# Issuing one batch's strided q, k and v two steps later on ScalarE's queue

## The chip, the core and the metric

The kernel runs on one core of a Trainium2 chip. The metric is the device time of one execution in microseconds (us), the median of several runs. TensorE does the matrix products, VectorE (DVE), ScalarE (ACT) and GpSimd (POOL) the rest; transfers are issued by SyncE (SP) and, for four of them in all, by ScalarE. Each engine works through its own instructions strictly in order and waits at an instruction until the semaphores that it names have been counted up.

## The reference, cut to what matters

Eight batches, eight heads, 576 tokens, head size 64. Heads 0 to 3 see the last 32 keys, heads 4 to 7 ("strided") every 32nd key. Attention is followed by a token mixer and a channel mixer with shared weights.

```python
scores = (q @ k.T) / 8
mask_local   = (rel >= 0) & (rel < 32)                    # heads 0-3
mask_strided = (rel >= 0) & (key % 32 == query % 32)      # heads 4-7
x = softmax(where(mask, scores, -1e9)) @ v                # [8, 576, 512]
h = relu(x.T @ w_tok1) @ w_tok2                           # token mixer
u = x + h.T
out = u + relu(u @ w_ch1) @ w_ch2                         # channel mixer
```

## The kernel before

Nearly all products are on TensorE in split precision: an operand is kept as a high and a low part, and three products stand for one. The channel mixer is done in nine groups. A group is one call of `mlp`: for 512 tokens of batch b it runs 12 up-projections (L688, 12 products each, into the tile `h`) and 12 down-projections (L700, 12 products each, into `acc`). Each of these 24 blocks ends with `done()`, which counts a step and then calls whatever was registered for that step with `at(step, function)`. All other work is hung on these steps, and so the order of the instructions on TensorE, VectorE, ScalarE and GpSimd is the order in which the program was written. SyncE's transfers are put in order by the builder, from its own estimate of when each could go.

What the first group (b = 0) carries beside its own blocks:

- `pieces`: most of the weights are still being loaded and split. A piece is a load of 512 KB into `w_raw` (two buffers) or `xhl` (L105, on SyncE's queue), two passes on ScalarE (L115, L118) and two on VectorE (L116, L120) which turn the int64 view into high and low words, then the high part on ScalarE (L129) and the low part on GpSimd (L130). The last six pieces use `w_raw` alone, so each of those loads waits until the piece two before it has been read.
- Batch 1's attention. Its strided heads write their results from `ex` (L361) and its local heads from `lx` (L245) to a tensor `x` in DRAM, `x_83` in the listings below.
- At step 12: `load_next`, which loads batch 1's `x` back into SBUF in six transfers, four for rows 0 to 511 (L452) and two for the rest (L455). At steps 15 to 19 the token mixer's first half follows: each chunk of `x` is cast on ScalarE (L466, into `xhl`), its low part taken on VectorE (L472, and L469 for the short last chunk), and multiplied on TensorE (L484).
- At step 12 as well: `first_ends`. It closes the pool of batch 1's attention, opens the pool `sp` in the same space, and starts the generator `strided` for batch 2. From batch 2 on the strided heads are done on GpSimd (products `sprod`, L372) and VectorE (sums, L418 and L442). The generator first issues the loads of k, q and v, 576 KB each, into three buffers `sa` (L385). For batch 2 alone they are issued from ScalarE's queue; for later batches from SyncE's. Their space was that of `ex`, `lx` and others, so the issue waits for those to be written out.
- From step 16: `some_strided`, which hands out GpSimd's products.

After each block's 12 up-projection products, ScalarE takes `gh` (L691) and VectorE `gl` (L692) out of `h`; there is one `h`, so the next up-projection waits for `gl`.

Transfers are counted on eight semaphores, named DMAHW0 to DMAHW7 in the listings. They are dealt in turn to the transfers of both queues in the order of the program, and a transfer waits until the one eight places before it has landed, unless something earlier has already waited for that.

Of the kernel before, what the change touches and what calls it, by code (L numbers as in the profile page):

```python
# [56 lines left out]
def attn_mixer_kernel(ctx, tc, qkT, vw, qs, ks, vs, qksT, vsP, mask, mask2, w1, w2, wt1, wt2, outT):  # L57
# [391 lines left out]
    def load_x(x_t, b, cs):  # L449
        src = xd[b // 2][S * (b % 2):S * (b % 2) + S, cs]  # L450
        for c in range(NSC - 1):
            nc.sync.dma_start(out=x_t[:, c, cs], in_=src[P * c:P * c + P])  # L452

        for r in range(2):
            nc.sync.dma_start(out=x_t[64 * r:64 * r + 64, NSC - 1, cs], in_=src[P * (NSC - 1):])  # L455
# [39 lines left out]
    def new_h(pool):  # L495
        return [[pool.tile([P, DM], F32R, name=f"h{k}{m}", bufs=1) for k in "hl"] for m in range(2)]
# [8 lines left out]
    def tok2(pool, ps_t, x_t, h, cc, us):  # L505

        cs = slice(P * cc, P * cc + P)
        pu = ps_t.tile([P, 512], F32, name="t")
        for c in range(NSC - 1):
            nc.tensor.matmul(pu[:, P * c:P * c + P], x_t[:, c, cs], ident, is_transpose=True, start=(c == 0), stop=False, skip_group_check=True)  # L510
        yield
        for m in range(2):
            hh, hl = h[m]
            for k, (l, r) in enumerate(((hh, t2h), (hh, t2l), (hl, t2h))):
                nc.tensor.matmul(pu, l[:, cs], r[:, m, :MAIN], start=False, stop=(m == 1 and k == 2), skip_group_check=True)  # L515
        us.append(split_u(pool, pu))
        yield
# [11 lines left out]
    def load_tails(u_t):  # L529

        halves = [xp.tile([P, 2, DM], F32, name="xhl") for _ in range(2)]
        for p in range(B // 2):
            l_t = halves[p // 2][:, p % 2]
            for b in (2 * p, 2 * p + 1):
                rs = slice(TAIL * (b % 2), TAIL * (b % 2) + TAIL)
                nc.sync.dma_start(out=u_t[rs, p], in_=ud[b][:TAIL])
                nc.sync.dma_start(out=l_t[rs], in_=ud[b][TAIL:])
            nc.gpsimd.tensor_tensor(out=u_t[:, p], in0=u_t[:, p], in1=l_t, op=ALU.add)

    def tail_u(pool, ps_t, u_t, cc):  # L540
        pu = ps_t.tile([P, 512], F32, name="t")
        for p in range(B // 2):
            nc.tensor.transpose(pu[:, P * p:P * p + P], u_t[:, p, P * cc:P * cc + P], ident)
        return split_u(pool, pu)
# [187 lines left out]
    def out_group(b):  # L732

        def write(cc, o_t, part):
            queue = nc.scalar if part.start else nc.sync
            queue.dma_start(out=outT[P * cc:P * cc + P, MAIN * b + part.start:MAIN * b + part.stop], in_=o_t[:, part])

        return write
# [14 lines left out]
    def first_ends():  # L753

        for g in lanes + rest:
            assert next(g, lanes) is lanes
        pools.pop("second").__exit__(None, None, None)
        pools["sp"] = ctx.enter_context(tc.tile_pool(name="sp", bufs=1, reuse_waits="tile"))
        turn["gen"] = strided(pools["sp"], NSB)
        turn["owed"] -= next(turn["gen"])  # L760

# [42 lines left out]
    for b in range(B):  # L804
        after = {}

        def at(i, f, *args):
            after.setdefault(i, []).append(lambda: f(*args))

        def load_next(b):  # L810
            x_t = xp.tile([P, NSC, DM], F32, name="x", bufs=1)
            x_next.update(x=x_t, h=new_h(xp), u=[])
            assert turn["batch"] > b or b < NSB, (b, turn)
            load_x(x_t, b, slice(0, DM))
            x_next["tok1"] = tok1(xp, ps_t, x_t, x_next["h"], slice(0, DM))


        def do_tok1():
            next(x_next["tok1"], None)

        def do_tok2(ccs):
            mixes = [tok2(up0, ps_t, x_next["x"], x_next["h"], cc, x_next["u"]) for cc in ccs]
            for g in mixes + mixes:
                next(g)

        def do_tail(cc):
            x_next["u"].append(tail_u(up0, ps_t, x_next["x"], cc))

        at(2 if b == 0 else 0, tok2_tail, ps_t, x_t, h, b)
        if b + 1 < B:  # L830
            at(12, load_next, b + 1)
            steps = (15, 16, 17, 18, 19, 19) if b < 2 else range(14, 20)
            for i in steps:
                at(i, do_tok1)
            for cc in (0, 2):
                at(20 + cc, do_tok2, (cc, cc + 1))
        else:
            x_next.update(x=xp.tile([P, NSC, DM], F32, name="x", bufs=1), u=[])
            at(1, lambda: load_tails(x_next["x"]))
            for cc in range(NCC):  # L840
                at(20 + cc, do_tail, cc)
        if b == 0:
            for i in range(len(pieces)):
                at(int(1.8 * i) / 2, do_pieces, i)
            for k, g in enumerate(lanes):
                for i in range(12):
                    at(i + 0.5 * k, next, g, None)
            for g, steps in zip(rest, ((0, 1.5, 2.5, 3.5), (2, 4.5, 5.5, 6.5), (5, 7.5, 8.5, 9.5), (7, 9.5, 10.5, 11.5)), strict=True):
                for i in steps:
                    at(i, next, g, None)  # L850
            at(12, first_ends)
            at(int(0.9 * len(pieces)) + 1, staging_ends)
        for k, steps in UNITS[b].items():
            for n, i in enumerate(steps):
                if i is not None:
                    at(i, unit, k, n)
        for i in range(24):
            if b or i >= 16:
                at(i, some_strided, 20 if b < 2 else 23)
        mlp(u, after, out_group(b))  # L860
        x_t, h, u = x_next["x"], x_next["h"], x_next["u"]
# [76 lines left out]
```

## Time and profile before

| | |
|---|---|
| median of 3 runs | 821.47 us (820.43 to 827.81) |
| the profiled execution | 818.1 us |
| its span, first to last instruction | 816.3 us |
| TensorE busy | 796.5 us (98%) |
| VectorE, GpSimd, ScalarE busy | 451.1, 410.7, 234.5 us |
| mean granted TensorE clock | 0.992 |

The profiled execution is 1.8 us longer than its span. Times inside the span are counted from its first instruction. A timeline line gives start, duration, engine, code line, operation, the tile written <- the tiles read, and in brackets the idle time before it and what ended that. "SPq" and "ACTq" are instructions that issue a transfer; their duration is that of the issue, not of the transfer.

### The profile page before, as it was taken

What the parts mean: (1) busy time and instruction counts of PE and PEld (TensorE: products, weight loads), DVE (VectorE), ACT (ScalarE), POOL (GpSimd) and SP (SyncE); (2) the same over time, 40 slices, a digit from 0 to 9 for tenths busy, and PEclk for the clock granted to TensorE, in tenths of its full rate; (3) what the DMA queues carried; (4) which work ended last, traced back from release to release, by engine and by line L of the source; (5) the groups of instructions that cost most, each with busy time, mean ns of one, the idle gap of its engine ahead of it and who ended that gap; (6) DMA issues with size and microseconds to landing.
All of it is one profiled execution on the core that took longest, in us unless ns stands there. A gap on an engine that the chain in (4) does not pass through costs nothing.

```text
span 816.3 us, 14373 instructions
## 1 busy us (share of the span) xinstructions
PE 796.5 (98%) x5819; PEld 647.2 (79%) x5823; DVE 451.1 (55%) x991; ACT 234.5 (29%) x491; POOL 410.7 (50%) x309
## 2 busy tenths in 40 slices
PE   9799997999999999999999999999999999999998
PEld 6578675878788888888888888888888888888886
DVE  6867744777587667665856565666562223113112
ACT  5667754232121212132213121322122121111110
POOL 2223334959896696668767866686830101302000
PEclk9999997999999999999999999999999999999999
DMA  9586554233602251137104400542032013001001
GB/s 308 167 274 219 172 174 158 82 136 103 210 1 94 73 180 30 65 93 241 51 13 146 159 30 1 175 160 85 1 94 81 5 46 123 0 1 53 1 0 52
DMA packets 56622, 82.77 MB, mean 101 GB/s; under 512 B 18292, under 2 KB 33396, under 8 KB 56556
## 3 DMA queue, kind: packets, MB, share of 16 engines
q1 hardware_dynamic: 55980, 79.95, 30.3%
q10 hardware_dynamic: 576, 1.90, 0.7%
q8 instruction: 46, 0.75, 0.4%
q14 instruction: 20, 0.16, 0.1%
HBM read 61.32 MB, written 20.38 MB: 100 GB/s over the span
## 4 chain that ended last, share of the span: by engine, by line
PE 89%; DVE 4%; DMA 3%; ACT 1%; issue 1%; SPq 1%; DVEq 0%; ACTq 0%
PE acc L700 34%; PE h L688 31%; PE t L484 6%; PE t L515 5%; PE t L688 3%; PE t L510 1%; DMA x<-x 1%; PE t L296 1%; PE t L268 1%; PE t L334 1%; PE t L524 1%; PE t L286 1%; DVE w_f L120 1%; DMA eqk<-in_qksT 1%; DMA w_raw<-in_w 1%
## 5 line engine op out<-in xcount | busy, mean ns | idle before, releaser
L372 POOL TENSOR_TENSOR sprod<-sa,ss 128x576 f32<-128x576 f32 (+8 forms) x108 | 153.2, 1449 | 75.5 <-issue 39.0
L692 DVE SCALAR_TENSOR_TENSOR gl<-h,gh 128x512 fp32r<-128x512 f32 x99 | 68.3, 690 | 202.6 <-ACT gh L691 202.6
L372 POOL TENSOR_TENSOR sprod<-sa 128x576 f32<-128x576 f32 (+8 forms) x108 | 160.5, 1515 | 33.6 <-DVE ss L418 11.2
L700 PE MATMUL acc<-gh,w2h 128*128 128x512 f32 x432 | 171.7, 397 | 0.0
L700 PE MATMUL acc<-gl,w2h 128*128 128x512 f32 x432 | 169.4, 392 | 0.0
L700 PE MATMUL acc<-gh,w2l 128*128 128x512 f32 x432 | 169.1, 391 | 0.0
L688 PE MATMUL h<-uh,w1h 128*128 128x512 f32 x396 | 157.8, 398 | 1.0 <-DVE gl L692 1.0
L688 PE MATMUL h<-ul,w1h 128*128 128x512 f32 x396 | 154.7, 391 | 0.0
L688 PE MATMUL h<-uh,w1l 128*128 128x512 f32 x396 | 154.5, 390 | 0.0
L691 ACT ACTIVATE gh<-h 128x512 fp32r<-128x512 f32 x99 | 59.1, 597 | 308.1 <-PE h L688 308.0
L372 POOL TENSOR_TENSOR ot<-uh,ul 128x512 f32<-128x512 f32 x36 | 50.3, 1406 | 94.9 <-DVE xhl L472 47.6
L700 PEld LDWEIGHTS acc<-gh,w2h 128*128 128x128 f32 x432 | 81.9, 189 | 17.4
L700 PEld LDWEIGHTS acc<-gh,w2l 128*128 128x128 f32 x432 | 81.8, 189 | 17.4
L700 PEld LDWEIGHTS acc<-gl,w2h 128*128 128x128 f32 x432 | 81.9, 190 | 16.7 <-DVE gl L692 0.3
L688 PEld LDWEIGHTS h<-uh,w1h 128*128 128x128 f32 x396 | 74.3, 188 | 18.1 <-DVE gl L692 1.8
L688 PEld LDWEIGHTS h<-ul,w1h 128*128 128x128 f32 x396 | 74.5, 188 | 15.9
L418 DVE TENSOR_REDUCE ss<-sprod 128x9 f32<-128x576 f32 (+8 forms) x108 | 80.0, 778 | 11.8 <-POOL sprod L372 11.6
L688 PEld LDWEIGHTS h<-uh,w1l 128*128 128x128 f32 x396 | 74.4, 188 | 14.5
L442 DVE TENSOR_REDUCE sa<-sprod 128x64 f32<-128x576 f32 (+8 forms) x108 | 79.4, 776 | 7.9 <-POOL sprod L372 7.8
L484 PE MATMUL t<-xhl,t1h 128*128 128x512 f32 x144 | 45.8, 404 | 7.0 <-ACT xhl L466 6.2
L502 DVE TENSOR_TENSOR ul<-t,uh 128x512 fp32r<-128x512 f32 x36 | 24.8, 690 | 48.7 <-ACT uh L501 48.5
L472 DVE TENSOR_TENSOR xhl<-x,xhl 128x512 fp32r<-128x512 f32 x32 | 36.9, 1173 | 12.9 <-ACT xhl L466 12.9
(123 smaller groups left out, 880.7 us busy)
## 6 DMA issues: line engine op xcount, KB each, us to landing
out_t<-ot SPq DMA_DIRECT2D x35, 256.0 KB
w_raw<-in_w SPq DMA_DIRECT2D x17, 512.0 KB
lqk<-in_qkT SPq DMA_DIRECT2D x20, 416.0 KB
lv<-in_vw SPq DMA_DIRECT2D x20, 390.0 KB
x<-x SPq DMA_DIRECT2D x28, 256.0 KB
xhl<-in_w SPq DMA_DIRECT2D x7, 512.0 KB
x<-lv SPq DMA_DIRECT2D x9, 384.0 KB
x<-sa SPq DMA_DIRECT2D x24, 144.0 KB
```

Source lines behind the costliest of these rows:

```text
L120: nc.vector.scalar_tensor_tensor(out=a, in0=a, scalar=3, in1=y, op0=ALU.logical_shift_left, op1=ALU.bitwise_xor)
L372: i = nc.gpsimd.tensor_tensor(op=op, **operands)
L418: nc.vector.tensor_reduce(out=s_t[:, i, :i + 1], in_=pr.rearrange("p (n d) -> p n d", d=D), axis=AX.X, op=ALU.add)
L442: nc.vector.tensor_reduce(out=o_t[:, i], in_=pr.rearrange("p (d n) -> p d n", n=i + 1), axis=AX.X, op=ALU.add)
L472: apart.append(nc.vector.tensor_tensor(out=xlo, in0=x, in1=xh.bitcast(F32), op=ALU.subtract))
L484: nc.tensor.matmul(ph[m], l[:, c, P * m:P * m + P], r, start=(c == 0 and k == 0), stop=(c == NSC - 1 and k == 1))
L502: nc.vector.tensor_tensor(out=ul, in0=pu, in1=uh.bitcast(F32), op=ALU.subtract)
L515: nc.tensor.matmul(pu, l[:, cs], r[:, m, :MAIN], start=False, stop=(m == 1 and k == 2), skip_group_check=True)
L688: nc.tensor.matmul(ph, l[:, cc, fs], r, start=(cc == 0 and k == 0), stop=(cc == NCC - 1 and k == 2))
L691: nc.scalar.activation(out=gh, in_=ph, func=AF.Relu)
L692: nc.vector.scalar_tensor_tensor(out=gl, in0=ph, scalar=0.0, in1=gh.bitcast(F32), op0=ALU.max, op1=ALU.subtract)
L700: nc.tensor.matmul(acc[cc], l[:, fc, cs], r, start=(fc == 0 and k == 0), stop=(fc == NFC - 1 and k == 2))
```

## The change

The generator for batch 2 is no longer started in `first_ends` at step 12 but in a function of its own at step 14. `first_ends` still closes and opens the pools at step 12.

```diff
@@ first_ends
         pools.pop("second").__exit__(None, None, None)
         pools["sp"] = ctx.enter_context(tc.tile_pool(name="sp", bufs=1, reuse_waits="tile"))
+
+    def first_strided():
         turn["gen"] = strided(pools["sp"], NSB)
         turn["owed"] -= next(turn["gen"])
@@ b == 0
             at(12, first_ends)
+            at(14, first_strided)
             at(int(0.9 * len(pieces)) + 1, staging_ends)
```

ScalarE's queue at that place before, around the three loads of k, q and v (`sa`); `w_raw`, `w_rest`, `w_f`, `w1h` and `w2h` belong to the pieces:

```order
L691 ACTIVATE gh<-h 128x512 [waits PE_49]
L385 DMA sa<-in_ks 128x1152 [waits DMAHW5_49]
L385 DMA sa<-in_qs 128x1152 [waits DMAHW0_49,DMAHW7_49,DVE_49,Activation_49]
L385 DMA sa<-in_vs 128x1152 [waits DMAHW3_49,DMAHW1_49]
L115 ACTIVATE w_rest_92<-w_raw,small 128x512 [waits DMAHW2_49]
L118 ACTIVATE w_f<-w_raw 128x512 [waits Pool_49]
```

ScalarE's queue around the same loads with the change, two steps on, where the next `gh` has been taken and the first cast of `x` (L466) follows:

```order
L691 ACTIVATE gh<-h 128x512 [waits PE_49]
L115 ACTIVATE w_rest_92<-w_raw,small 128x512 [waits DMAHW4_49,Activation_49]
L118 ACTIVATE w_f<-w_raw 128x512 [waits Pool_49]
L129 CAST w1h<-w_f 128x2x256 [waits DVE_49]
L385 DMA sa<-in_ks 128x1152
L385 DMA sa<-in_qs 128x1152 [waits DMAHW5_49,DMAHW0_49]
L385 DMA sa<-in_vs 128x1152 [waits DMAHW6_49,DMAHW3_49]
L466 CAST xhl<-x 128x512 [waits DMAHW3_49]
```

The three loads moved behind nine instructions of the pieces and one `gh`, and now stand directly ahead of the cast. The semaphores that they wait for changed with the place: DMAHW5 and DMAHW6 are now also those of the loads of `x`'s second and third chunk.

SyncE's queue around the loads of batch 1's `x`, the difference (- before, + with the change):

```order
 L245 DMA x_83<-lx 128x2x128
-L452 DMA x<-x_83 128x512 x4
+L452 DMA x<-x_83 128x512
+L105 DMA w_raw<-in_w 128x1024
+L452 DMA x<-x_83 128x512 x3
 L455 DMA x<-x_83 64x512 x2
-L105 DMA w_raw<-in_w 128x1024 x4
+L105 DMA w_raw<-in_w 128x1024 x3
```

The first of the last four weight loads moved from behind all six loads of `x` to behind the first of them. On TensorE, VectorE and GpSimd no instruction moved.

## Rows read from the trace of the kernel before

**Rows 1.** The page: TensorE's clock, in tenths, in 40 slices of 20.4 us.

```profile
PEclk9999997999999999999999999999999999999999
```

**Rows 2.** Waits of TensorE from 120 us to the end: total us, times, longest.

```profile
PE t L484 <- ACT xhl L466: 6.2, 2, 6.0
PE h L688 <- DVE gl L692: 1.0, 2, 0.6
```

**Rows 3.** Timeline of TensorE around the two longest of these waits.

```profile
122.32 0.50 PE L688 MATMUL h<-uh,w1h 128*128 128x512 f32 x1 [0.57 <-DVE gl L692]
...
124.94 0.39 PE L688 MATMUL h<-ul,w1h 128*128 128x512 f32 x1
131.32 0.80 PE L484 MATMUL t<-xhl,t1h 128*128 128x512 f32 x1 [5.99 <-ACT xhl L466]
```

**Rows 4.** Timeline of ScalarE, its issues among them.

```profile
115.56 0.38 ACTq L385 DMA_DIRECT2D sa<-in_ks  x1
...
116.95 0.34 ACTq L385 DMA_DIRECT2D sa<-in_vs  x1
117.35 0.88 ACT L115 ACTIVATE w_rest<-w_raw,small 128x512 uint8<-128x512 uint8 x1 [3.14 <-DMA x<-lx]
...
120.93 0.61 ACT L691 ACTIVATE gh<-h 128x512 fp32r<-128x512 f32 x1
128.86 0.87 ACT L115 ACTIVATE w_rest<-w_raw,small 128x512 uint8<-128x512 uint8 x1 [7.32 <-DMA w_raw<-in_w]
...
130.64 0.62 ACT L466 CAST xhl<-x 128x512 fp32r<-128x512 f32 x1
```

**Rows 5.** Timeline of SyncE's issues.

```profile
116.98 3.55 SPq L452 DMA_DIRECT2D x<-x  x4
120.58 3.91 SPq L455 DMA_DIRECT2D x<-x  x2
124.59 9.92 SPq L105 DMA_DIRECT2D w_raw<-in_w  x4
...
130.26 0.33 SPq L105 DMA_DIRECT2D w_raw<-in_w  x1
```

**Rows 6.** The chain that ended last: start, us, what.

```profile
116.98 6.99 DMA x<-x
...
124.59 4.18 DMA w_raw<-in_w
...
131.32 2.93 PE t L484 x6
134.25 4.34 PE acc L700 x12
138.59 1.37 PE t L484 x6
...
144.04 2.72 PE acc L700 x12
```

**Rows 7.** Windows: length, busy PE PEld DVE ACT POOL, PEclk, DMA share, GB/s.

```profile
99.00:102.00 3.00, 1.24 (x39) 0.90 (x39) 2.90 (x9) 2.43 (x5) 1.38 (x2) 1.00 0.13 20
...
104.00:106.00 2.00, 2.00 (x8) 1.60 (x7) 0.89 (x2) 1.43 (x3) 0.00 (x0) 0.50 0.07 16
...
122.00:125.00 3.00, 2.68 (x12) 2.17 (x12) 0.26 (x1) 0.00 (x0) 1.10 (x1) 1.00 1.00 358
...
131.00:137.00 6.00, 5.68 (x13) 4.46 (x14) 4.52 (x5) 3.85 (x8) 4.08 (x3) 0.50 0.52 173
...
133.00:134.00 1.00, 1.00 (x3) 0.76 (x3) 1.00 (x1) 0.00 (x0) 0.79 (x1) 0.50 0.00 0
```

**Rows 8.** Timeline of GpSimd (first strided product), VectorE and TensorE (last chunk).

```profile
141.08 1.60 POOL L372 TENSOR_TENSOR sprod<-sa 128x576 f32<-128x576 f32 x1
...
146.57 0.69 DVE L469 TENSOR_TENSOR xhl<-x,xhl 64x512 fp32r<-64x512 f32 x1
...
147.51 1.07 PE L484 MATMUL t<-xhl,t1h 128*128 128x512 f32 x4
```

## The prediction

> **What bounds the kernel now.** I read the page first: TensorE is busy for 98% of the span (the table), and its clock is at full level everywhere but in the seventh slice, 122 to 143 us [rows 1]. So time can come only from the few gaps of TensorE and from that slice. The waits of TensorE say where the gaps are: after 120 us it waits 6.2 us in all for the cast of `x` (6.0 at once) and 1.0 us for `gl` [rows 2]. Its timeline puts both big ones beside each other: 0.57 us before the up-projection at 122.32, and 5.99 us before the first token-mixer product at 131.32 [rows 3]. Both lie where the change works, so I went back from them on ScalarE and then on SyncE.
>
> The small one: the up-projection waits for `gl`, this for `gh`, which ScalarE takes only at 120.93. Ahead of `gh` stand six instructions of the pieces, which begin at 117.35 after 3.14 us in which ScalarE issued the three strided loads and waited for the `lx` write to land [rows 4]. The large one: the cast at 130.64 stands behind a piece (L115 at 128.86) that waited 7.32 us for its `w_raw` [rows 4]. That load was issued only at 124.59, since SyncE had all six loads of `x` to issue first, from 116.98 on, and the last two took it 3.91 us [rows 5]. The chain shows why: it waited for a load of `x` issued at 116.98 to land after 6.99 us [rows 6]. A `w_raw` of twice that size landed after 4.18 us [rows 6]; the load of `x` was so slow because the three strided loads (1.77 MB) had been issued just before it and the 16 DMA engines were fully busy (share 1.00, 358 GB/s from 122 to 125) [rows 7]. After the long gap the granted clock is 0.50 from 131 to 137, the lower of its two levels, 1.2 GHz [rows 7].
>
> **The change, part by part.**
>
> *1. The small gap goes.* ScalarE is free from 117.35 - 3.14 = 114.21 instead of 117.35 [rows 4]. The six piece instructions took 120.93 - 117.35 = 3.6 us, so they end near 118, and `gh` can go up to 3.1 us earlier, as soon as its products are through; `gl` follows 0.57 us too late now, so a fifth of that is enough. Worth 0.57 us [rows 3]; bounds 0, if a `w_raw` is late, and 0.57.
>
> *2. The large gap shrinks.* With the change SyncE issues one load of `x` at about 117.0 and then the `w_raw`, at 116.98 + 0.4 = 117.4. Its buffer is free by then, because ScalarE's two passes over the old contents now begin at 114.2 and take under a us each (0.88 for the first) [rows 4]. It lands 4.18 us later at the slow end [rows 6]; at the quick end, the `w_raw` issued at 130.26 [rows 5] had no traffic left in the window 133 to 134 [rows 7], so about 3.1 us. That gives 120.5 to 121.6; I take 121.0, nearer the quick end, because only one 256 KB load goes ahead of it. From the landing at 128.78 (124.59 + 4.18) to the cast at 130.64 it was 1.86 us [rows 4, 6]. Now the three issues stand in between: 117.35 - 115.56 = 1.79 us before, with a wait for `lx` in it; three issues of 0.34 to 0.38 us without one are 1.1. I take 1.4. TensorE began 0.68 us after the cast [rows 3, 4]. Sum: 121.0 + 1.86 + 1.4 + 0.68 = 124.9; bounds 120.5 + 1.86 + 1.1 + 0.68 = 124.1 and 121.6 + 1.86 + 1.8 + 0.68 = 125.9. TensorE's last product before it ends at 124.94 + 0.39 - 0.57 = 124.8, so it waits 0.1 us instead of 5.99, at worst 1.1. The token mixer starts 131.32 - 124.9 = 6.4 us earlier (5.4 to 6.5), part 1 included; part 2 alone is 5.8.
>
> *3. The clock stays up.* With no long gap there is no reason for the lower level. At it, six token-mixer products took 2.93 us against 1.37 later, and twelve down-projection products 4.34 against 2.72 [rows 6]: 1.56 + 1.62 = 3.2 us, all of it on TensorE's path, with nothing else waiting there. So 6.4 + 3.2 = 9.6 us by the second token-mixer block.
>
> *4. Something of it is given back.* ScalarE's and VectorE's work on the pieces does not run faster with TensorE's clock. It is moved by the 6.4 us of the cast, and by some more where it waited for TensorE, while TensorE would gain 9.6. The tightest place is the last chunk of `x`: VectorE makes it by 146.57 + 0.69 = 147.26, and the pair of products on it begins half way through the four at 147.51, near 148.0 [rows 8]. That is a slack of 0.7 us. VectorE gets there between 6.4 and 9.6 us earlier; I take the middle, 8.0, since on the way the casts wait in turn for the pieces and for TensorE to free `xhl`. So TensorE can be 8.0 + 0.7 = 8.7 ahead: 0.9 us given back. Bounds: nothing, and 6.4 + 0.7 = 7.1 ahead, 2.5 given back.
>
> *5. What must not become late.* The strided loads now go out near 123 instead of 115.6 to 117.3. GpSimd wants k and q for its first product at 141.08 [rows 8], with the change some 8 us earlier, near 133. If they took as long as the slow load of `x`, 6.99 us [rows 6], they would land near 130.5. Hidden, 2 us to spare; v is wanted much later. The three remaining `w_raw`s share the DMA engines with them, but each is also issued earlier, as SyncE is through with `x` near 121, without the wait in its last two issues, instead of at 120.58 + 3.91 = 124.5 [rows 5]. From then to the end TensorE never waits longer than 0.6 us [rows 2], so nothing in the rest takes the gain back, as long as batch 2's strided chain moves with it, which part 4 covers.
>
> Sum: 0.6 + 5.8 + 3.2 - 0.9 = 8.7 us of the 816.3 us span. The profiled execution, 818.1 with the 1.8 us around its span, becomes 809.4; the median of the runs shown, 3.4 us above it, 821.47 - 8.7 = **812.8**. That is 1.06% less.
>
> The Trainium skill ("DMA: Bandwidth & Descriptors", section "Issuing engines are not separate DMA queues") says that transfers issued by any engine run on the same 16 DMA engines and interleave, and that another issuing engine saves only issue time. The trace agrees in the full DMA share at 122 to 125 while both queues had transfers under way. By this rule the 1.77 MB are only moved, not saved: the gain would last just as far as what they now push back is less urgent than the loads of `x` were, and otherwise it would be rival (b), at 817.5.
>
> **The rivals.** *(a) The gap is halved, not closed.* If the `w_raw` lands at the slow end and the three issues wait for the second and third chunk of `x`, TensorE stands still for 1 to 2 us. A gap of that size cost the clock once: in the window 99 to 102 TensorE was busy for only 1.24 of 3 us, and from 104 to 106 the clock is 0.50 [rows 7]. Price: 1.5 us of gap and, over those 2 us and some on either side at half clock, another 1.5: 8.7 - 3.0 = 5.7, so 815.8. For it: the issues now stand right ahead of the cast. Against: by part 2 there is a us of room.
>
> *(b) The strided bytes push the next weights.* 1.77 MB at 358 GB/s [rows 7] are 4.9 us of all DMA engines. If they go ahead of the second `w_raw` (wanted by ScalarE near 125 for the piece that stands ahead of the next `gh` and the next casts), that piece comes at up to 130, and TensorE waits some 3.5 us at its second block, with part of the half clock: 3 to 5 us are left, 817.5. Against: SyncE issues that load near 121, before the strided ones.
>
> *(c) It does not do what it says.* Only if the order of the `w_raw` load gave nothing, the 0.57 us would be left: 820.9. The large wait is plainly for that load, so I hold this unlikely.
>
> *(d) Slower.* The third strided issue waits for the third chunk of `x`, and every cast and `gh` stands behind it on ScalarE. The cast is as late as before when that issue goes at 130.64 - 0.4 = 130.2, and beyond this each us costs TensorE one us. To be slower by 8.2 us, the chunk, issued near 118.7, would have to land at 138, 20 us later, where the slowest took 6.99 [rows 6]. With a price of 8.2: 829.7.
>
> **How the numbers follow.** The forecast, 8.7 us with bounds 7.1 and 9.6 from part 4 (811.9 to 814.4, and 810 to 816 with the scatter of a us or two that medians have): 0.66. (a) 0.18, (b) 0.10, (c) 0.03, (d) 0.03, each with its price as above. One per cent is 8.2 us, about what a measurement of this kernel can tell from no change, and the limit, 813.3, runs through the forecast's own range: of its 0.66 I count 0.50 as faster by over 1% and 0.16 as less; add 0.02 of (a) whose price may be smaller. So faster 0.52, within 1% 0.45, slower 0.03. The range goes from 809.5, a full 9.6 with some scatter, to 818.5, which takes in (a) and (b).
>
> **What would show it.** Right: ScalarE works on pieces from 114.2 without a gap, its three issues stand after 122 and take under 2 us; one `w_raw` is issued near 117.4; the first token-mixer product starts near 125; the clock is 1.00 from 120 to 150; the last product's start is some 9 us earlier. Part 4 would show as a gap of TensorE before the last chunk's products or the first token-mixer output after it. Wrong would be the forecast if the clock falls although the gap is under 1 us, if TensorE waits for `gl` or for casts between 126 and 137, or if GpSimd's first product waits for a strided load and the loads of batch 2's `x`, near 208 then, are late by it.

## The result, and the profile after

The change makes the kernel faster: 812.38 us (median of 6 runs, 811.70 to 813.23) against 820.16 us (818.53 to 827.81) beside it, a ratio of 0.9895, 95% interval 0.9856 to 0.9933. The profiled execution took 813.02 us, its span 811.2 us.

Two traces are compared from a common point. The same `gh` (L691), just ahead of the place of the change, starts at 113.61 in the trace before and at 114.81 after, though nothing ahead of it changed; over all runs of this study it lay between 113.3 and 115.0. So 1.20 us are taken off every time of the trace after, before it is set against one of before ("aligned"). The two lines, before and after:

```profile
113.61 0.60 ACT L691 ACTIVATE gh<-h 128x512 fp32r<-128x512 f32 x1 [1.45 <-PE h L688]
```

```profile
114.81 0.60 ACT L691 ACTIVATE gh<-h 128x512 fp32r<-128x512 f32 x1 [1.45 <-PE h L688]
```

The page after: TensorE's clock in 40 slices, which answers to [rows 1].

```profile
PEclk9999999999999999999999999999999999999999
```

The low slice is gone. The two largest waits of TensorE from 120 us on (total, times, longest) answer to [rows 2]:

```profile
PE t L484 <- DVE xhl L469: 1.1, 1, 1.1
PE t L484 <- ACT xhl L466: 0.8, 2, 0.5
```

The 6.2 us for the cast are 0.8, and there is a new wait of 1.1 us for VectorE's part of the last chunk of `x`. TensorE's timeline shows where they lie, from the up-projection at which the small gap was to the first down product of the token mixer (L515):

```profile
123.03 0.50 PE L688 MATMUL h<-uh,w1h 128*128 128x512 f32 x1
...
126.16 0.73 PE L484 MATMUL t<-xhl,t1h 128*128 128x512 f32 x2
...
131.04 0.73 PE L484 MATMUL t<-xhl,t1h 128*128 128x512 f32 x2 [0.49 <-ACT xhl L466]
...
141.94 0.73 PE L484 MATMUL t<-xhl,t1h 128*128 128x512 f32 x2 [1.09 <-DVE xhl L469]
...
146.53 0.66 PE L510 MATMUL t<-ident,x 128*128 128x128 f32 x4 [0.22 <-DVE hl L493]
146.94 0.47 PE L515 MATMUL t<-t2h,hh 128*128 128x512 f32 x1
```

The second block and L515 in the trace before:

```profile
138.43 0.62 PE L484 MATMUL t<-xhl,t1h 128*128 128x512 f32 x2
...
152.39 0.48 PE L515 MATMUL t<-t2h,hh 128*128 128x512 f32 x1
```

The gap of 0.57 us [rows 3] is gone at 123.03. The first token-mixer product starts at 126.16 (124.96 aligned) instead of 131.32 [rows 3], 6.4 us earlier. The second block starts at 131.04 (129.84) instead of 138.43, 8.6 us earlier. But L515 is only 6.65 us earlier. So 1.9 us are given back between 131 and 147.

ScalarE and SyncE after, where they answer to [rows 4] and [rows 5]:

```profile
121.66 0.59 ACT L691 ACTIVATE gh<-h 128x512 fp32r<-128x512 f32 x1
123.00 0.89 ACT L115 ACTIVATE w_rest<-w_raw,small 128x512 uint8<-128x512 uint8 x1 [0.75 <-DMA w_raw<-in_w]
...
124.09 0.38 ACTq L385 DMA_DIRECT2D sa<-in_ks  x1
...
125.05 0.39 ACTq L385 DMA_DIRECT2D sa<-in_vs  x1
...
125.48 0.62 ACT L466 CAST xhl<-x 128x512 fp32r<-128x512 f32 x1 [0.58 <-DMA x<-x]
128.09 0.89 ACT L115 ACTIVATE w_rest<-w_raw,small 128x512 uint8<-128x512 uint8 x1 [1.99 <-DMA w_raw<-in_w]
```

```profile
118.54 0.38 SPq L105 DMA_DIRECT2D w_raw<-in_w  x1
118.98 1.37 SPq L452 DMA_DIRECT2D x<-x  x3
...
121.63 8.20 SPq L105 DMA_DIRECT2D w_raw<-in_w  x3
```

The weight load that was issued at 124.59 [rows 5] goes out at 118.54, and ScalarE reads it at 123.00. The loads of `x` take SyncE 1.4 and 1.1 us instead of 3.55 and 3.91; the strided loads are no longer ahead of them. The next weights, issued at 121.63, are waited for 1.99 us.

What gives the time back stands on VectorE, and beside it on GpSimd:

```profile
134.65 1.37 DVE L472 TENSOR_TENSOR xhl<-x,xhl 128x512 fp32r<-128x512 f32 x1 [1.21 <-ACT xhl L466]
135.95 1.69 DVE L116 TENSOR_SCALAR w_rest<-w_raw 128x512 uint8<-128x512 uint8 x1
137.53 1.76 DVE L120 SCALAR_TENSOR_TENSOR w_f<-w_f,w_rest 128x512 uint32<-128x512 uint32 x1
...
141.20 0.69 DVE L469 TENSOR_TENSOR xhl<-x,xhl 64x512 fp32r<-64x512 f32 x1
```

```profile
135.74 1.57 POOL L372 TENSOR_TENSOR sprod<-sa 128x576 f32<-128x576 f32 x1
137.28 1.47 POOL L372 TENSOR_TENSOR ot<-uh,ul 128x512 f32<-128x512 f32 x1
```

The two passes on the piece (L116, L120) take 0.46 and 0.67 us one piece earlier (132.43 and 132.78), where GpSimd is idle. But they were as long in the trace before:

```profile
140.70 0.69 DVE L472 TENSOR_TENSOR xhl<-x,xhl 128x512 fp32r<-128x512 f32 x1 [1.91 <-ACT xhl L466]
141.31 1.71 DVE L116 TENSOR_SCALAR w_rest<-w_raw 128x512 uint8<-128x512 uint8 x1
142.90 1.76 DVE L120 SCALAR_TENSOR_TENSOR w_f<-w_f,w_rest 128x512 uint32<-128x512 uint32 x1
```

So they are not a new cost of the change; they are a stretch of VectorE's way to the last chunk which a faster TensorE does not shorten. New is the pass ahead of them, L472: it starts 7.25 us earlier than before (aligned), takes 1.37 us instead of 0.69, because it now falls beside a low part of the weights on GpSimd (L130, 134.18 to 135.47), and what follows is 6.6 us earlier. GpSimd's first product of batch 2 is 6.5 us earlier than in [rows 8] (141.08 against 134.54 aligned), and VectorE's part of the last chunk 6.6 (146.57 against 140.00).

### The profile page after: what moved, and what is told of

It reads as the page before. It is cut to its first block, busy times and chain, and to the rows that moved or that the text cites. A ratio compares the mean times of both kernels' runs of the same rounds, so it can differ in the third digit from the quotient of the medians.

```text
span 811.2 us, 14379 instructions
## 1 busy us (share of the span) xinstructions
PE 795.3 (98%) x5819; PEld 644.9 (79%) x5823; DVE 452.6 (56%) x991; ACT 234.9 (29%) x491; POOL 410.6 (51%) x309
## 4 chain that ended last, share of the span: by engine, by line
PE 85%; DVE 3%; DMA 3%; issue 1%; POOL 1%; ACT 1%; SPq 0%; DVEq 0%; POOLq 0%; ACTq 0%
PE acc L700 34%; PE h L688 31%; PE t L515 5%; PE t L484 5%; PE t L688 3%; DMA w_raw<-in_w 2%; PE t L510 1%; PE t L296 1%; PE t L268 1%; PE t L524 1%; PE t L286 1%; DMA x<-x 1%; POOL sprod L372 1%; DVE w_rest L116 1%; PE t L334 1%
## 5 line engine op out<-in xcount | busy, mean ns | idle before, releaser
L691 ACT ACTIVATE gh<-h 128x512 fp32r<-128x512 f32 x99 | 59.0, 596 | 307.7 <-PE h L688 307.6
L418 DVE TENSOR_REDUCE ss<-sprod 128x9 f32<-128x576 f32 (+8 forms) x108 | 80.0, 778 | 12.7 <-POOL sprod L372 12.4
L472 DVE TENSOR_TENSOR xhl<-x,xhl 128x512 fp32r<-128x512 f32 x32 | 37.2, 1182 | 13.1 <-ACT xhl L466 13.1
```

Source lines behind the costliest of these rows:

```text
L418: nc.vector.tensor_reduce(out=s_t[:, i, :i + 1], in_=pr.rearrange("p (n d) -> p n d", d=D), axis=AX.X, op=ALU.add)
L472: apart.append(nc.vector.tensor_tensor(out=xlo, in0=x, in1=xh.bitcast(F32), op=ALU.subtract))
L691: nc.scalar.activation(out=gh, in_=ph, func=AF.Relu)
```

## The experiments

The ratios are to the kernel before, run beside each on the same chip; the changed kernel's is 0.9895. The diffs are cut to the lines that matter.

**1. The clock alone.** The kernel before, with 22 idle products put into the up-projection ahead of the long gap, so that TensorE keeps its clock and starts the token mixer no earlier.

```diff
+    fill = lambda: (idle := ps_t.tile([P, 512], F32, name='t'), [nc.tensor.matmul(idle, w1h[:, 0, :P], w1h[:, 1, :512], start=True, stop=True) for _ in range(22)])
-            at(12, first_ends)
+            at(12, first_ends); at(15.5, fill)
```

> The kernel before, with 22 idle products (their result is thrown away) put in the middle of the up-projection ahead of the long gap, so that TensorE works through most of it and keeps its clock. The casts of x are as late as before. Theory A, the prediction's sum (the clock's 3.2 us lie on TensorE's path and only 0.9 us are given back): 2.3 to 3.2 us faster than before. Theory B (from the casts on, ScalarE and VectorE set the pace, and what TensorE gains by its clock it waits at the later chunks): 0.5 to 1.3 us faster, with the clock at 1.00 and new waits of TensorE for the casts or for the last chunk of some 2 us.

Measured: 819.21 us, ratio 0.9976 (0.9949 to 1.0003). TensorE's timeline:

```profile
124.03 5.17 PE L803 MATMUL t<-w1h 128*128 128x512 f32 x22
...
132.21 0.73 PE L484 MATMUL t<-xhl,t1h 128*128 128x512 f32 x2 [1.64 <-ACT xhl L466]
...
137.28 0.73 PE L484 MATMUL t<-xhl,t1h 128*128 128x512 f32 x2 [0.20 <-ACT xhl L466]
...
148.19 0.73 PE L484 MATMUL t<-xhl,t1h 128*128 128x512 f32 x2 [1.07 <-DVE xhl L469]
```

The clock was 1.0 throughout and the first pair of products took 0.73 us instead of 1.22. Counted from its own `gh` (113.86), the first token-mixer product came 0.6 us later than before, since the weight load landed later in this run. The second block still came 1.4 us sooner (23.42 us after `gh` against 24.82), and then TensorE stood 1.07 us for the last chunk, as in the changed kernel. From the first token-mixer product to L515 it took 20.97 us, before 21.07. So in the trace the clock by itself bought 0.1 us, which speaks for theory B. The times do not decide: the interval of the ratio, 0.2 us slower to 4.2 us faster, takes in theory A as well.

**2. The strided loads on SyncE's queue**, at step 12 of the kernel before. The builder then sets them behind the first of the late weight loads and the loads of `x`.

```diff
-        queue = nc.scalar if b == NSB else nc.sync
+        queue = nc.sync
```

> The kernel before, with batch 2's three strided loads issued from SyncE's queue, still at step 12. ScalarE's queue is free of them; the builder puts them behind all six loads of x and puts the weight load behind the first load of x, as in the changed kernel. If what counts is that x and the first weight load go ahead of the strided loads, it is as fast as the change (7 to 9 us under before). If the strided loads hurt the second weight load, which here stands behind them in the same queue, it is 3 to 5 us under before, with ScalarE waiting for that weight load until about 133.

Measured: 817.08 us, ratio 0.9970 (0.9950 to 0.9991). SyncE, ScalarE and TensorE:

```profile
122.18 0.43 SPq L385 DMA_DIRECT2D sa<-in_vs  x1
...
124.24 9.74 SPq L105 DMA_DIRECT2D w_raw<-in_w  x3
...
132.25 0.87 ACT L115 ACTIVATE w_rest<-w_raw,small 128x512 uint8<-128x512 uint8 x1 [8.03 <-DMA w_raw<-in_w]
...
135.19 1.22 PE L484 MATMUL t<-xhl,t1h 128*128 128x512 f32 x2 [6.01 <-ACT xhl L466]
```

The cast is as early as with the change (123.59), but the second weights go out behind the three strided loads, are read 8.0 us later, and the long gap moves to the second block. This is rival (b) of the prediction, made real; 2.3 us of gain are left between the medians (819.40 and 817.08), a little less than the 3 to 5 that I had expected.

**3. One step earlier.** The changed kernel with `at(13, first_strided)`; the orders of SyncE and the other engines stay as with step 14.

> The change with the three loads issued one step earlier, at step 13: SyncE's order is that of the changed kernel, but the strided loads go out some 5 us earlier, together with the loads of x. If SyncE's order (the weight load ahead of five loads of x) makes the gain, it is as fast as the change, 7 to 9 us under before. If the strided traffic ahead of x and the weight load makes it, the first cast is 3 to 4 us later than with the change and the time is 3 to 5 us under before.

Measured: 816.36 us, ratio 0.9965 (0.9947 to 0.9982).

```profile
116.36 0.39 ACTq L385 DMA_DIRECT2D sa<-in_ks  x1
...
117.75 0.38 SPq L105 DMA_DIRECT2D w_raw<-in_w  x1
...
126.12 0.87 ACT L115 ACTIVATE w_rest<-w_raw,small 128x512 uint8<-128x512 uint8 x1 [5.97 <-DMA w_raw<-in_w]
...
128.58 1.22 PE L484 MATMUL t<-xhl,t1h 128*128 128x512 f32 x2 [3.66 <-ACT xhl L466]
```

With the strided loads ahead of it, the weight load is read 8.4 us after its issue (126.12 - 117.75), with the change 4.5 (123.00 - 118.54). So SyncE's new order is not enough: what counts as well is that the strided traffic starts after that load. A part of the loss is the clock, which was 0.60 from 126 to 131 here, after the gap of 3.66 us.

**4. GpSimd out of the way.** The changed kernel, with GpSimd's products of batch 2 from step 18 instead of 16, handed out faster to make up for it.

```diff
-            if b or i >= 16:
-                at(i, some_strided, 20 if b < 2 else 23)
+            if b or i >= 18:
+                at(i, some_strided, 18 if b == 0 or b == 1 and i < 12 else 20 if b < 2 else 23)
```

> The change, with GpSimd's products for batch 2 begun at step 18 instead of 16, after the last low parts of the weights, and handed out a little faster then. In the changed kernel VectorE's passes on the last pieces take 1.7 us instead of 0.5 to 0.7 while GpSimd multiplies. If this stretching is what holds back the last chunk of x, TensorE's wait of 1.1 us there goes and the time is 1 to 2 us under the change. If it is the weight loads that come last, nothing moves there. If batch 2's strided result then comes late for its load near 207, it is slower than the change by 1 to 3 us.

Measured: 812.97 us, ratio 0.9916 (0.9886 to 0.9946). VectorE and TensorE:

```profile
136.52 0.67 DVE L120 SCALAR_TENSOR_TENSOR w_f<-w_f,w_rest 128x512 uint32<-128x512 uint32 x1
...
144.41 0.48 PE L515 MATMUL t<-t2h,hh 128*128 128x512 f32 x1
...
212.16 0.50 PE L688 MATMUL h<-uh,w1h 128*128 128x512 f32 x1 [1.65 <-DVE gl L692]
...
230.93 0.73 PE L484 MATMUL t<-xhl,t1h 128*128 128x512 f32 x2 [1.44 <-DVE xhl L469]
```

The pass takes 0.67 us again, the wait for the last chunk is gone, and L515 comes 2.7 us sooner than with the change (144.41 - 114.97 = 29.44 us after its `gh`, against 32.13). Not all of this is the edit's. The second block, which lies ahead of anything that the edit moves, was already 1.0 us sooner here, because the second weights landed sooner. From the second block to L515 it took 14.2 us against 15.9, so the edit is worth 1.7. That holds in the other traces too: 14.2 us in experiments 6, 10, 11 and 12, which contain this edit, 15.8 to 15.9 in experiments 1, 5, 7 and 8, which do not, 15.2 in experiment 9. All of it is lost again in two waits, at 212 and 231.

**5. and 6. Less work in GpSimd's chain.** Two blocks of batch 2's scores left out, products and sums (so part of the scores is not computed), of the changed kernel and of experiment 4.

```diff
         def qk(i, pr):
-            n = i + 1
+            n = 0 if b == NSB and i in (3, 13) else i + 1
+            if n == 0: return
```

> The changed kernel, with the products on GpSimd and the sums on VectorE of two of batch 2's score blocks (i = 3 and 13) left out: part of the scores is not computed. It takes about 2.7 us of products from GpSimd's strided chain and puts nothing in their place. Theory C (the end of that chain sets the time; up to about 147 us TensorE, which waits 1.09 us for the last chunk of x, is late as well): the last product with v on GpSimd ends 1.5 to 2.7 us sooner, at 199.3 to 200.5 instead of 202.0, the span ends as much sooner, and the time is 809.7 to 810.9 us (ratio to the changed kernel 0.997 to 0.998). Rival R1 (the chain on GpSimd only follows; TensorE's own work and waits set the pace, with the chain's end at a constant distance from the end for another reason): the chain ends sooner and the span does not, 812.0 to 812.8 us.

> The kernel in which GpSimd's products of batch 2 start two steps later, with the same two score blocks left out (part of the scores is not computed). There TensorE was 2.9 us ahead at the first down product (144.4 instead of 147.2) and lost it again by waits of 1.7 and 1.4 us after 150 us. Theory C: the chain ends 2.0 to 2.7 us sooner, at 199.1 to 199.8, the waits after 150 us shrink, and the time is 809.5 to 811.0 us. Rival R1 (TensorE's waits after 150 us come from VectorE's own passes, whatever GpSimd's chain does): the waits stay and the time is 812.0 to 813.0 us.

Measured: 813.49 us, ratio 0.9926 (0.9896 to 0.9955), and 813.43, ratio 0.9932 (0.9910 to 0.9954).

Neither got faster; theory C fell in the form in which I had put it, and rival R1 with it, which also had the chain end sooner. GpSimd was idle for 8.4 us ahead of its products with v in the changed kernel anyway, and for 8.6 in experiment 5. From L515 to the first of these products it is 29.8 us in both traces, so the left-out scores shifted nothing; in experiments 4 and 6 it is 32.1 and 31.9. That experiment 5 has them 1.2 us later after its `gh` than the changed kernel (63.17 against 61.94) comes from ahead of the edit: there the cast of `x` waited 1.94 us for its load, and L515 was 1.2 us late as well. The products with v are released by the softmax on VectorE, and that stands at a fixed place in VectorE's order, between the `gl` of TensorE's blocks. So the chain is tied to TensorE's steps.

**7. and 8. The strided bytes.** One load instead of three (q and v of batch 2 are then other data), and all three with v's issued six steps later.

```diff
-        q_t, k_t, v_t = operand(), operand(), operand()
+        q_t, k_t, v_t = [operand()] * 3 if b == NSB else (operand(), operand(), operand())
-        for t, src in ((k_t, ks), (q_t, qs), (v_t, vs)):
+        for t, src in ((k_t, ks), (q_t, qs), (v_t, vs))[:1 if b == NSB else 3]:
```

> The changed kernel, in which batch 2 loads k alone and uses it in the place of q and v as well (the scores and sums of that batch are of other data), so that the strided traffic of this place is a third. Theory S (the strided bytes delay the second load of raw weights, which took 6.38 us and landed at 128.0): it lands by 126 us, the cast of x's second chunk and the second block of products come 1 to 3 us sooner, and the time is 810.0 to 812.0 us. Rival X (the bytes of x and of the four weight loads themselves fill the transfers there): the second load lands within 0.7 us of 128.0 and the time is 812.0 to 813.0 us.

```diff
+        loads = [lambda t=t, src=src: queue.dma_start(out=t, in_=src[b].rearrange("p a b -> p (a b)")) for t, src in ((k_t, ks), (q_t, qs), (v_t, vs))]
+        v_late.append(loads.pop()) if b == NSB else None; [f() for f in loads]
...
+            at(14, first_strided); at(20, lambda: v_late.pop()())
```

> The changed kernel with v's strided load alone issued six steps later, on the same queue, ahead of its use at 176 us. Theory S: a third of the strided bytes no longer lies beside the second load of raw weights, which lands 0.7 to 1.5 us sooner than 128.0; the time is 811.0 to 812.0 us. Rival X: it lands within 0.5 us of 128.0, and the time is 812.0 to 812.8 us. If the issue of 0.4 us at the later place holds up ScalarE, 812.5 to 813.5 us.

Measured: 812.31 us, ratio 0.9923 (0.9903 to 0.9943), and 812.57, ratio 0.9917 (0.9892 to 0.9941). The second weight load in the chain that ended last (start, duration), with the change, in experiment 7 and in 8:

```profile
121.63 6.38 DMA w_raw<-in_w
```

```profile
120.50 6.28 DMA w_raw<-in_w
```

```profile
120.54 6.29 DMA w_raw<-in_w
```

They land at 128.01, 126.78 and 126.83; `gh` was at 114.81, 113.64 and 113.68 in these runs, so 13.2, 13.1 and 13.2 us after it. Two thirds of the strided bytes less save the load nothing that could be told from its scatter: in the seven other traces with the change's order of loads, all three strided loads behind it, it took 5.3 to 7.6 us. The two edited versions were timed within theory X's range, and theory S, which had the load land 0.7 to 2 us sooner, is not borne out. What makes the load slow is then most likely what is already under way when it is issued, the first weights and the loads of `x`: with one strided load instead of three the DMA engines were as full from 120.5 to 126.8 (share 1.03 against 1.01). The strided loads come only 2.5 us behind it. A version with fewer bytes ahead of it was not tried.

**9. and 10. GpSimd's last product with v left out** (2.48 us; the sum on VectorE reads v in its place, so batch 2's last block is other data), of the changed kernel and of experiment 4.

```diff
         def av(i, pr):
             n = i + 1
-            on_gpsimd(
+            b == NSB and i == 17 or on_gpsimd(
...
-            nc.vector.tensor_reduce(out=o_t[:, i], in_=pr.rearrange("p (d n) -> p d n", n=i + 1), axis=AX.X, op=ALU.add)
+            nc.vector.tensor_reduce(out=o_t[:, i], in_=v_t if b == NSB and i == 17 else pr.rearrange("p (d n) -> p d n", n=i + 1), axis=AX.X, op=ALU.add)
```

> The changed kernel with the last product with v of batch 2 on GpSimd (i = 17, 2.48 us) left out; the sum on VectorE stays and reads v in its place, so that batch's last block of the output is of other data. Theory C2 (from the first down product on TensorE has next to no waits in the changed kernel, 0.39 us at 175 and 0.34 us at 217, and sets the pace itself; GpSimd's chain of batch 2 is not late there): the chain ends 2.5 us sooner and the time stays within 0.7 us of the changed kernel, 811.7 to 812.9 us. Rival G (the end of GpSimd's products with v, which lies 609 us ahead of the end in every kernel so far, sets the time): 809.7 to 810.7 us.

> The same product left out of the kernel in which GpSimd's products of batch 2 start at step 18 (the last block of that batch's output is of other data). There TensorE came 2.7 us sooner to its first down product than in the changed kernel and lost 1.65 us at 212, for a half that stood on VectorE behind a sum that waited for GpSimd's next product, and 1.45 us at 231. Theory C2 (GpSimd's chain of batch 2 is late only here, and its lateness is handed on through VectorE's order): the wait at 212 goes or shrinks to under 0.5 us and the time is 809.9 to 811.6 us, 1.2 to 2.5 us under 812.97. Rival V (VectorE's own stretched passes at 215 to 230 set the time): the waits move to 220 to 231 and the time is 812.3 to 813.0 us.

Measured: 818.43 us, ratio 0.9968 (0.9937 to 0.9999), and 817.62, ratio 0.9973 (0.9948 to 0.9999): 5 to 6 us slower than the kernels without this edit, which no theory had. My edit did a second thing. The sum now held v's buffer until VectorE came to it, and q of batch 3 is loaded into that buffer; the builder then also set that load behind the four stores of the strided result on SyncE's queue (204.56 to 206.71). The changed kernel first, then experiment 9 (SyncE, GpSimd, TensorE):

```profile
202.11 0.33 SPq L385 DMA_DIRECT2D sa<-in_qs  x1
...
206.22 4.20 POOL L372 TENSOR_TENSOR sprod<-sa 128x576 f32<-128x576 f32 x3 [2.59 <-DVE sa L442]
```

```profile
206.80 0.59 SPq L385 DMA_DIRECT2D sa<-in_qs  x1
...
211.88 4.14 POOL L372 TENSOR_TENSOR sprod<-sa 128x576 f32<-128x576 f32 x3 [11.56 <-DMA sa<-in_qs]
...
217.53 0.80 PE L688 MATMUL h<-uh,w1h 128*128 128x512 f32 x1 [4.69 <-DVE gl L692]
```

So the mishap is a measurement: q of batch 3 issued 5.1 us later, counted from each kernel's `gh`, costs TensorE a wait of 4.69 us, through GpSimd's products, the sums that wait for them on VectorE, and the `gl` behind those sums. Behind that wait the clock was 0.61 from 218 to 225, which adds to the loss. In experiment 10 q was 4.2 us later than in experiment 4, and the wait there grew from 1.65 to 6.2 us. In the changed kernel q goes out when GpSimd's products with v end (202.09), and TensorE waits nowhere behind it for longer than 0.34 us. As a test of C2 against G the pair says nothing.

**11. That product on VectorE instead**, in experiment 4; everything is computed.

```diff
+    def vec(op, **operands):
+        nc.vector.tensor_tensor(op=op, **operands)
-            on_gpsimd(
+            (vec if b == NSB and i == 17 else on_gpsimd)(
```

> The kernel in which GpSimd's products of batch 2 start at step 18, with the last product with v of batch 2 (i = 17) on VectorE instead of GpSimd; everything is computed. Theory C2: GpSimd is free 2.5 us sooner, VectorE has one pass of 1.2 to 2.5 us more at about 200, where it is busy for six tenths, and the time is 810.0 to 811.8 us, faster than both kernels. Rival V: VectorE's longer queue holds up the low half of the up-projection there as much as GpSimd's chain did, 812.5 to 814.0 us.

Measured: 814.37 us, ratio 0.9918 (0.9886 to 0.9950), no better than experiment 4. q of batch 3 goes out no earlier (201.48, which is 87.6 us after `gh`, in experiment 4 86.9), since VectorE comes to the product late and takes 3.31 us for it (198.10 to 201.41), where I had expected 1.2 to 2.5. TensorE waits 1.51 us at 206.10 for `gl` behind it, and 1.98 at 216.53 for the cast of `x`.

**12. q of batch 3 in three pieces**, the rows that are read first ahead, in experiment 4; everything is computed.

```diff
-            queue.dma_start(out=t, in_=src[b].rearrange("p a b -> p (a b)"))
+            for lo, hi in ((4, 13), (13, NJ), (0, 4)) if src is qs and b > NSB else ((0, NJ),):
+                queue.dma_start(out=t[:, lo * D:hi * D], in_=src[b].rearrange("p a b -> p (a b)")[:, lo * D:hi * D])
```

> The kernel in which GpSimd's products of batch 2 start at step 18, with q of batch 3 and later loaded in three pieces, the rows that the first five steps of products read ahead of the rest; everything is computed. In all kernels so far q of batch 3 is issued when GpSimd's last product with v of batch 2 frees a tile, takes 4.1 to 5.1 us to land, and GpSimd's first product of batch 3 starts with the landing. Theory C3 (this load, handed on through GpSimd's products, the sums in VectorE's order and the low half of the up-projection, is what TensorE waits 1.65 us for at 212): the first product starts 1.0 to 2.5 us after less, the wait at 212 shrinks to under 0.8 us, and the time is 810.8 to 812.3 us, under both kernels. Rival D (the transfers are busy there with the next x, and half of the rows lands no sooner than the whole): 812.5 to 813.5 us. Rival V (VectorE's passes at 215 to 231, stretched while GpSimd multiplies, set the time): the wait at 212 shrinks, that at 231 grows by as much, 812.3 to 813.0 us.

Measured: 813.91 us, ratio 0.9914 (0.9881 to 0.9947). SyncE, GpSimd, ScalarE and TensorE:

```profile
201.07 0.81 SPq L386 DMA_DIRECT2D sa<-in_qs  x2
...
204.31 4.20 POOL L372 TENSOR_TENSOR sprod<-sa 128x576 f32<-128x576 f32 x3 [1.70 <-issue]
...
210.02 0.50 PE L689 MATMUL h<-uh,w1h 128*128 128x512 f32 x1 [0.29 <-DVE gl L693]
...
215.07 0.62 ACT L467 CAST xhl<-x 128x512 fp32r<-128x512 f32 x1 [7.42 <-DMA x<-x]
...
215.74 0.73 PE L485 MATMUL t<-xhl,t1h 128*128 128x512 f32 x2 [2.70 <-ACT xhl L467]
```

GpSimd starts 3.2 us after the issue instead of 4.6 in experiment 4, and the wait of 1.65 us at 212 falls to 0.29, as theory C3 had it. The time does not follow: TensorE now waits 2.70 us for the landing of batch 2's `x`, whose strided half is what the products with v have just made. Neither rival had this wait.

## Why the prediction came out

The forecast of 812.8 us was met (812.38), and each mechanism was there, but the sum was too high in one term, part 4, and two others came out right by errors that cancelled. Point by point:

- **Part 1**, 0.57 us: the size as put, the way not. The pieces did not end near 118: VectorE's passes on one of them took 1.5 and 1.8 us beside GpSimd, and ScalarE waited 1.82 us for them. `gh` came at 121.66, 120.46 aligned, 0.5 us earlier than before and not up to 3.1. It was just enough: no gap is listed at 123.03.
- **Part 2**, first product at 124.9: it came at 124.96 aligned, and that it came so near is luck. The load was issued as forecast (118.54, 117.34 aligned), but ScalarE's wait for it ended only at 123.00 (121.80), so it landed some 0.7 us later than the 121.0 of the sum and just outside its bounds. The quick end of these was misread besides: with no traffic left in 133 to 134, a load issued at 130.26 had taken at most 2.7 us, not 3.1. The three issues took 125.05 + 0.39 - 124.09 = 1.35 us (I took 1.4), but they lay mostly beside ScalarE's own passes, so from reading the load to the cast it was 2.48 us against 1.78 before: 0.7 more, where the sum had 1.4. In the seven other traces with this order of loads the first product came 10.7 to 12.4 us after `gh`, here 11.35. Experiment 3 shows the cause: with the strided loads ahead of that weight load the cast is at 127.91, 13.85 us after `gh`, with the change at 125.48, 10.67 after it.
- **Part 3**, 3.2 us by the second block: 8.6 - 6.4 = 2.2 us of it arrived; half of the rest is the wait of 0.49 us for the cast there. That wait is, in small, one of the signs that the prediction named for being wrong.
- **Part 4** is the term that was mis-sized: 0.9 us given back was forecast, from 9.6 to 8.7, with 2.5 as the bound, and L515 started 6.65 us earlier, so 2.95 from the 9.6, outside that bound. The place was right, the last chunk of `x`. Two numbers failed. VectorE was to get there "the middle, 8.0" us earlier; it got there 6.57 us earlier (146.57 against 140.00), near the low end of 6.4. And the slack of 0.7 us did not last: the products on the last chunk came 7.2 us earlier, but L510 behind them then waited for VectorE once more (`hl`, 0.22 us, line 146.53 above), and L515 is left with 6.65. The chain that ended last in the changed kernel runs here from the second weight load, which took 6.38 us and which no part of the sum had priced, through ScalarE, GpSimd and at last VectorE's `hl` to L510. VectorE's passes on the last piece but one take 1.7 us instead of 0.5 to 0.7 in both kernels, L472 ahead of them is stretched as well with the change, and no faster TensorE moves those. Experiment 1 shows it from the other side (in its trace the clock is given back whole), and experiment 4 by taking part of the cause away: with GpSimd's products later, the stretch from the second block to L515 is 1.7 us shorter.
- **Part 5**: as put. GpSimd's first product at 135.74 waits for no transfer, and no cost of the strided bytes to the second weights could be told from the scatter (experiments 7 and 8). The bound that I named there was "as long as batch 2's strided chain moves with it": with the change it does move with it. The times after each kernel's own `gh`:

| kernel | first down product (L515) | products with v begin | from there to the end of the span |
|---|---|---|---|
| before | 38.78 | 68.61 | 634.1 |
| experiment 1, idle products | 39.32 | 69.14 | 634.4 |
| experiment 2, SyncE's queue | 37.46 | 67.28 | 634.1 |
| experiment 3, step 13 | 35.71 | 65.51 | 633.8 |
| the change | 32.13 | 61.94 | 634.5 |
| experiment 7, one load | 31.97 | 61.80 | 634.3 |
| experiment 8, v later | 32.07 | 61.89 | 635.5 |
| experiment 5, fewer scores | 33.36 | 63.17 | 634.1 |
| experiment 4, GpSimd at 18 | 29.44 | 61.55 | 634.6 |
| experiment 6, fewer scores | 30.64 | 62.55 | 634.8 |
| experiment 12, q in pieces | 30.30 | 62.43 | 635.5 |

The last column varies by 1.7 us, while the start of the products with v varies by 7.6. (In experiments 9 to 11 the products themselves or q of batch 3 behind them are changed, and it is 637 to 641.) From first down product to the end it is 663.6 to 665.4 us in the first eight rows, but 666.7 to 667.6 in the last three: TensorE, 2 us sooner there without the products with v, gains nothing. This does not show that these products bound the changed kernel, where TensorE waits at most 0.39 us behind L515: the edit of experiment 4 itself sets them 2.3 us later behind L515, and no version has both sooner. What follows those products is shown for two paths, q of batch 3 (experiments 9, 10 and 12) and batch 2's `x` (experiment 12). Why GpSimd's idle 5.3 to 8.6 us ahead of them is not used, was read from VectorE's order and not tried: the softmax would have to be handed out a block earlier.

The match of the median is partly luck: the traces give 6.65 us at L515 and 5.1 + 1.2 = 6.3 over the aligned span, the runs 7.8 us with an interval of 5.5 to 11.8, and the kernel before had a median 1.3 us lower in these runs than in those that the forecast started from. Beside the experiments its median was 819.0 to 820.6 us.

- **Rival (b)** did not come, since SyncE had issued the second weights at 121.63, 2.5 us ahead of the strided loads; experiment 2 shows its price when the order is the other way. A weight load on SyncE's queue was read 8.4 us after its issue behind strided loads on ScalarE's (experiment 3), 4.5 us ahead of them. The rule of the Trainium skill ("DMA: Bandwidth & Descriptors", section "Issuing engines are not separate DMA queues"), that transfers of all queues share the same 16 engines, agrees with that. **Rival (a)**: the gap left was 0.5 us at most, and the clock stayed. **(c)** and **(d)** have nothing for them.

No version tried beats the changed kernel: those that compute everything and contain the change at step 14 (experiments 4, 8, 11, 12) lie at 0.9914 to 0.9918, inside its interval.

## What to carry to other kernels

A large background load belongs behind the small loads on which the next stage waits, whatever queue issues it: here one step, 13 or 14, decided whether a weight load was read 8.4 or 4.5 us after its issue. When a gap of the bounding engine closes, do not add the clock's gain to it before you have followed the helpers' own chain through the same stretch, with durations as long as they are while a second helper works beside them; the gain is what the slowest chain moves. And before a product or a buffer's last reader is moved or taken out, look who loads into that buffer next.

## What was not expected of the hardware

Some of VectorE's passes are stretched while GpSimd is at work: 0.46 to 1.69 us (L116), 0.67 to 1.76 us (L120) and 0.69 to 1.37 us (L472) in the changed kernel, and back to 0.67 us for the same L120 in experiment 4, where GpSimd's `sprod` products come later. It looks less like a slower pass than like one that waits for GpSimd's instruction beside it: these three end 0.3 to 0.6 us after it does (L116 at 137.64 after `sprod` at 137.31, L120 at 139.29 after `ot` at 138.75, L472 at 136.02 after the low part at 135.47). Not every pass is caught: `gl` at 130.51 takes 0.69 us beside a low part on GpSimd. And 1.77 MB of strided loads issued 2.5 us behind a 512 KB load did not slow it by anything that shows (6.38 us, and 6.28 with a third of the bytes), while the same loads issued 1.4 us ahead of a like load nearly doubled the time to its reading.
